# Linear attention, routed experts and a gated layer on one core: the state's product and expert 0's rounding on POOL, sums of decays three units ahead

## The chip, the cores and the metric

The kernel runs on one core of a Trainium2 chip. The metric is device time in microseconds (us), the median of three runs. Five engines work in parallel, each in the order of its own queue: PE (matrix products), DVE (vector work), ACT (functions of one input, copies), POOL (a slower vector engine that also issues indirect transfers) and SP, which only issues transfers. An instruction waits on semaphores for what it reads and for the buffer that it writes.

## The reference

Three layers follow each other; each works on 3072 tokens of 384 numbers.

```python
# 1: linear attention, B=4, H=8, S=768, D=48
f = 1.0 / (1.0 + np.exp(-f_logit))
for t in range(S):
    state = f[:, :, t, :, None] * state + np.einsum('bhd,bhe->bhde', k[:, :, t], v[:, :, t])
    y[:, :, t] = np.einsum('bhd,bhde->bhe', q[:, :, t], state)
# 2: each token goes to the one expert e of 8 with the largest logit
h = np.maximum(x[mask] @ w1[e], 0.0)
out[mask] = gate_w[mask, None] * eom[mask, e, None] * (h @ w2[e])
# 3: gated layer, 1536 wide
out = ((1.0 / (1.0 + np.exp(-(x @ w_gate)))) * (x @ w_val)) @ w_out
```

## The kernel before

**Stages.** The attention is cut into 24 units u of 128 tokens (6 units for each of 4 batches; `c = u % 6` is the place in the batch). After it come nine passes over the experts (expert 0 in two, the second when its late rows have arrived) and then six groups of the gated layer. The order of all engines' work is written out by hand (`manual_schedule`).

**One unit.** The decays `ft` go through Exp and Ln on ACT (`s_log`, `s_log2`), then through a running sum along the tokens on DVE (`s_sum`, L556). `s_keys` takes Exp of the sum on ACT (`gi`, L565) and multiplies the keys by it on DVE (`kT`, L567); `s_queries` takes Exp of the negative sum on ACT (L574) and multiplies the queries by it on POOL (`qT`, L576). `s_end` copies the chunk's whole decay to `gc_all` (L581). `s_score` makes the scores `pS` on PE from kT and qT, `s_mask` masks them on DVE in two halves (`am`, L607), `s_y` makes the output `pY` on PE from am, v, qT and the state, and ACT copies it to `xT`. `s_turn` turns kT on PE (`pk`, copied to `kt` by ACT), `s_state` makes `pM` from kt and v on PE, and DVE adds the old state (L637) and multiplies by the chunk's decay (L638): this is the next state `sn`, made for c = 1 to 4 in these two steps (16 units) and for c = 0 in one (L635). `s_rows` turns xT back on PE (`px`), ACT copies it to rows `x`, and DVE sums the router's logits (`lg`, L505).

**The loop.** Iteration i, from 1 to 23, issues, in this order: scores of unit i, keys and queries of i+1, the load of qk for i+4, `s_end`, rows that POOL puts into the experts' places (`put_rows`, two or three indirect transfers, L385), Exp of the decays of i+2, the load of ft for i+6, masks of i, a step of the routing (`step_route`), output of i-1, Ln of i+2, the load of v for i+4, the state of i, the sum of i+2, the turn of i+1, a step of `feed`, the rows of i-1.

**Loads.** SP issues them in the loop's order: per unit two of qk (48x1024 floats, 192 KB each), two of ft (48x512, 96 KB each) and one of v (128x384, 192 KB). There are 3 buffers of qk, 4 of ft, 5 of v. In iterations 2 to 5 SP also writes two blocks of zeros (`xs_all<-zrow`). `feed` loads expert 0's weights, five tiles ahead (128x512 or 128x2x384 floats: three of 256 KB and two of 384 KB first, from iteration 6), and `split` makes of each 128x512 or 128x384 piece a rounded half `w_hi` on ACT (L243) and the rest `w_lo` on DVE (L244); the loop makes one of the 14 pieces in each iteration from 8 on.

**After the loop.** `make_plan`, a generator of five steps, sorts the experts by size on DVE and PE (L895 to L935); the passes' loop calls it from unit 2 on. Its second step holds a product on PE (`pf`, L904) that reads `chk` of the first. Only then are the next expert's weights loaded.

The two lines that the change moves between engines:

```python
    nc.scalar.copy(hi, src)                                                     # L243, in split
    nc.vector.tensor_tensor(out=sn, in0=sn, in1=gcb, op=ALU.mult)               # L638, in s_state
```

## Time and profile before

| | us |
|---|---|
| runs | 850.44, 854.07, 851.29 |
| median | 851.29 |
| the profiled execution | 854.3 |
| its span, first to last instruction | 852.5 |

The profile is of one execution, 3.0 us above the median; 1.8 us of its time lie around its span. PE is busy for 823.2 us of the span, DVE for 450.2, ACT for 353.5, POOL for 166.9. The attention takes the first 142 us. After that PE is busy in nearly every microsecond, so what moves the end is when PE can begin with the experts, and waits of PE behind that. Times in rows count from the span's start.

### The profile page before, as it was taken

The page shows a single profiled execution, that of the slowest core. Times are in us where ns is not written, and L with a number is a line of the kernel's source. Part 1 is how long each engine was busy: PE and PEld are TensorE (multiplying, and loading weights), DVE is VectorE, ACT ScalarE, POOL GpSimd, SP SyncE. Part 2 cuts the span into 40 slices and gives each one's busy share as a digit, 9 for nine tenths or more (in the row PEclk, how much of TensorE's full clock was granted, in tenths as well). Part 3 has the DMA queues.
Part 4 walks back from the last instruction along what each step waited for, and adds up shares of the span by engine and source line. Part 5 has one row for each costly group of instructions (what it writes and reads, how often), then busy time and mean ns, then how long its engine had stood idle before and what let it go on. Part 6 is the DMA issues. An engine that isn't in the chain of part 4 may idle for free.

```text
span 852.5 us, 13950 instructions
## 1 busy us (share of the span) xinstructions
PE 823.2 (97%) x5289; PEld 727.7 (85%) x5289; DVE 450.2 (53%) x896; ACT 353.5 (41%) x738; POOL 166.9 (20%) x172
## 2 busy tenths in 40 slices
PE   8898989999999999999999999999999999999995
PEld 5776777998899999998888888888888888888884
DVE  6787997568878988997552213222222221232211
ACT  7677874375556665654342212212221221122211
POOL 4225475102323333332000100100010010001001
PEclk9999999999999999999999999999999999999999
DMA  6999762666667767634000200110020010001001
GB/s 158 258 283 266 192 177 82 217 208 196 208 191 224 222 212 218 204 104 139 1 1 1 74 1 1 38 38 0 1 75 1 0 38 2 1 1 38 1 1 40
DMA packets 51645, 87.56 MB, mean 103 GB/s; under 512 B 12874, under 2 KB 32754, under 8 KB 51570
## 3 DMA queue, kind: packets, MB, share of 16 engines
q1 hardware_dynamic: 44946, 62.97, 26.0%
q0 software_dynamic: 6624, 23.62, 8.6%
q8 instruction: 43, 0.70, 0.4%
q14 instruction: 32, 0.26, 0.1%
HBM read 68.35 MB, written 18.22 MB: 102 GB/s over the span
## 4 chain that ended last, share of the span: by engine, by line
issue 51%; PE 32%; DMA 6%; DVE 4%; ACT 3%; POOL 2%; SPq 0%; POOLq 0%; DVEq 0%; ACTq 0%
PE ph L812 5%; PE po L812 5%; PE po L814 5%; PE po L813 5%; PE ph L813 4%; PE ph L814 4%; DMA qk<-in_qkt_dram 4%; POOL out_dram L1022 2%; DMA xs_all<-zrow 1%; DMA ft<-in_ft_dram 1%; PE ptx L430 1%; DVE ls L556 1%; PE pY L653 1%; ACT gi L565 1%; PE px L494 1%
## 5 line engine op out<-in xcount | busy, mean ns | idle before, releaser
L1150 DVE TENSOR_TENSOR hf<-pv,sg 128x512 f32<-128x512 f32 x72 | 49.8, 692 | 266.7 <-PE pv L814 263.1
L1146 ACT ACTIVATE sg<-pg 128x512 f32<-128x512 f32 x72 | 43.1, 598 | 172.8 <-PE pg L814 172.8
L1153 ACT CAST hh<-hf 128x512 fp32r<-128x512 f32 x72 | 44.7, 620 | 161.1 <-DVE hf L1150 152.2
L1022 POOL DMA_INDIRECT out_dram<-ob,ids x24 | 23.6, 983 | 411.4 <-DVE ob L1021 405.9
L813 PE MATMUL po<-w_lo,hh 128*128 128x384 f32 x288 | 96.6, 335 | 0.0
L812 PE MATMUL po<-w_hi,hh 128*128 128x384 f32 x288 | 96.4, 335 | 0.0
L814 PE MATMUL po<-w_hi,hl 128*128 128x384 f32 x288 | 96.3, 334 | 0.0
L814 PE MATMUL pg<-xt_hi,w_lo 128*128 128x512 f32 x216 | 85.5, 396 | 0.0
L813 PE MATMUL pv<-xt_lo,w_hi 128*128 128x512 f32 x216 | 85.5, 396 | 0.0
L812 PE MATMUL pg<-xt_hi,w_hi 128*128 128x512 f32 x216 | 85.5, 396 | 0.0
L813 PE MATMUL pg<-xt_lo,w_hi 128*128 128x512 f32 x216 | 85.1, 394 | 0.0
L812 PE MATMUL pv<-xt_hi,w_hi 128*128 128x512 f32 x216 | 85.1, 394 | 0.0
L814 PE MATMUL pv<-xt_hi,w_lo 128*128 128x512 f32 x216 | 85.1, 394 | 0.0
L244 DVE TENSOR_TENSOR w_lo<-st,w_hi 128x384 fp32r<-128x384 f32 (+1 forms) x112 | 68.9, 647 | 13.9 <-ACT w_hi L243 13.2
L1154 DVE TENSOR_TENSOR hl<-hf,hh 128x512 fp32r<-128x512 f32 x72 | 49.9, 693 | 49.4 <-ACT hh L1153 49.4
L812 PE MATMUL po<-hh,w_hi 128*128 128x192 f32 (+8 forms) x216 | 74.2, 343 | 0.0
L814 PE MATMUL po<-hh,w_lo 128*128 128x192 f32 (+8 forms) x216 | 74.1, 343 | 0.0
L813 PE MATMUL po<-hl,w_hi 128*128 128x192 f32 (+8 forms) x216 | 73.9, 342 | 0.0
L812 PE MATMUL ph<-xt_hi,w_hi 128*128 128x304 f32 (+7 forms) x192 | 67.9, 354 | 0.9 <-DVE hl L1073 0.9
L193 POOL TENSOR_SCALAR cva<-cva 128x512 f32<-128x512 f32 (+1 forms) x30 | 56.3, 1875 | 62.4 <-ACT cva L192 62.1
L1072 ACT ACTIVATE hh<-ph 128x192 fp32r<-128x192 f32 (+8 forms) x72 | 35.6, 494 | 79.1 <-PE ph L814 73.3
L243 ACT CAST w_hi<-st 128x384 fp32r<-128x384 f32 (+1 forms) x112 | 59.3, 558 | 21.9 <-PE po L813 20.0
(173 smaller groups left out, 1658.1 us busy)
## 6 DMA issues: line engine op xcount, KB each, us to landing
st<-in_moe_w_dram SPq DMA_DIRECT2D x48, 256.0 KB
st<-in_moe_w_dram SPq DMA_DIRECT2D x32, 384.0 KB
qk<-in_qkt_dram SPq DMA_DIRECT2D x48, 192.0 KB
ft<-in_ft_dram SPq DMA_DIRECT2D x48, 96.0 KB
v<-in_v_dram SPq DMA_DIRECT2D x24, 192.0 KB
stg<-in_moe_w_gate_dram POOLq DMA_DIRECT2D x9, 512.0 KB
stg<-in_moe_w_val_dram POOLq DMA_DIRECT2D x9, 512.0 KB
stg<-in_moe_w_out_dram POOLq DMA_DIRECT2D x12, 384.0 KB
```

The source lines that it names most:

```text
L193: nc.gpsimd.tensor_scalar(out=af, in0=af, scalar1=HW_LEAST, scalar2=HW_MOST, op0=ALU.max, op1=ALU.min)
L243: nc.scalar.copy(hi, src)
L244: nc.vector.tensor_tensor(out=lo, in0=src, in1=hi.bitcast(F32), op=ALU.subtract)
L812: nc.tensor.matmul(ps, lhsT=ah, rhs=bh, start=first, stop=False)
L813: nc.tensor.matmul(ps, lhsT=ah, rhs=bl, start=False, stop=False)
L814: nc.tensor.matmul(ps, lhsT=al, rhs=bh, start=False, stop=last)
L1022: put = nc.gpsimd.indirect_dma_start(out=out[:, :], out_offset=bass.IndirectOffsetOnAxis(ap=idx[g][:, i : i + 1], axis=0), in_=ob, in_offs ...
L1072: nc.scalar.activation(out=hh, in_=pS, func=AF.Relu)
L1146: nc.scalar.activation(out=sg, in_=pg, func=AF.Sigmoid)
L1150: nc.vector.tensor_tensor(out=hf, in0=pv, in1=sg, op=ALU.mult)
L1153: nc.scalar.copy(hh, hf)
L1154: nc.vector.tensor_tensor(out=hl, in0=hf, in1=hh.bitcast(F32), op=ALU.subtract)
```

## The change

It does these things:

- `s_state`: the product L638 goes from DVE to POOL; the add in front of it stays on DVE.
- `split` gets `steps`. For expert 0 (`r == 0`) it hands back two steps: POOL rounds `w_hi` (instead of ACT), and DVE makes `w_lo` in a later call of `feed.step`. The loop calls two steps in an iteration from 8 on, one in iteration 7.
- `feed.issue()`, the first load of weights, moves from iteration 6 to 5.
- Exp, Ln and running sum work in place in one tile `ls` with four buffers, and from iteration 4 on they run for unit i+3 instead of i+2; iteration 4 does both. The load of ft follows the Exp directly, so that from iteration 4 on it is for i+7.
- `s_end` is for i+1, so that the decay is there when POOL multiplies.
- In the last iteration a step of routing stands ahead of the masks, and the two others behind the rows of unit 22.
- `make_plan` starts one unit of the passes later (no step in unit 2, one in unit 3, then two).

```diff
-            ln = wk.tile([PD, HP, P], F32, name="ln")
-            nc.scalar.activation(out=ln, in_=tin["f", u], func=AF.Exp, scale=-1.0)
+            ls = wk.tile([PD, HP, P], F32, name="ls", bufs=4)
+            nc.scalar.activation(out=ls, in_=tin["f", u], func=AF.Exp, scale=-1.0)
+            load("f", u + NFT)
...
+            (nc.scalar.copy if steps == 1 else nc.gpsimd.tensor_copy)(hi, src)
...
-                    nc.vector.tensor_tensor(out=sn, in0=sn, in1=gcb, op=ALU.mult)
+                    nc.gpsimd.tensor_tensor(out=sn, in0=sn, in1=gcb, op=ALU.mult)
...
-                on(s_end, i)
+                on(s_end, i + 1)
+                if 1 < i <= LEAD:
+                    s_log(i + 2)
+                    s_log2(i + 2)
...
-                if i > 1:
-                    on(s_log, i + 2)
-                    s_mask(i, 0)
-                load("f", i + 6)
+                if i >= LEAD:
+                    on(s_log, i + 3)
+                if i == LAST:
+                    step_route()
+                s_mask(i, 0)
...
-                if i > 1:
-                    on(s_sum, i + 2)
+                if i >= LEAD:
+                    on(s_sum, i + 3)
                 on(s_turn, i + 1)
-                if i == 6:
+                if i == 5:
                     feed.issue()
-                if i >= 8:
-                    feed.step(1)
+                if i >= 7:
+                    feed.step(1 if i == 7 else 2)
...
-                        for _ in range(1 if i == 2 else 2):
+                        for _ in range(min(i - 2, 2)):
```

What stands in a row on the engines, at three places. First SP's queue in iterations 5 to 7, before; `qk_114` is the buffer of unit 9, `qk_115` that of unit 10, `qk_116` that of unit 11.

```order
L539 DMA qk_114<-in_qkt_dram 48x1024 x2
L539 DMA ft_113<-in_ft_dram 48x512 x2
L535 DMA v<-in_v_dram 128x384
L784 DMA xs_all<-zrow 128x2x386 x2
L539 DMA qk_115<-in_qkt_dram 48x1024 x2
L539 DMA ft_110<-in_ft_dram 48x512 x2
L535 DMA v<-in_v_dram 128x384
L252 DMA st_748<-in_moe_w_dram 128x512
L252 DMA st_750<-in_moe_w_dram 128x512
L252 DMA st_752<-in_moe_w_dram 128x512
L259 DMA st_754<-in_moe_w_dram 128x2x384
L259 DMA st_756<-in_moe_w_dram 128x2x384
```

And the same place after:

```order
L555 DMA qk_114<-in_qkt_dram 48x1024 x2
L555 DMA ft_110<-in_ft_dram 48x512 x2
L551 DMA v<-in_v_dram 128x384
L264 DMA st_665<-in_moe_w_dram 128x512
L264 DMA st_667<-in_moe_w_dram 128x512
L264 DMA st_669<-in_moe_w_dram 128x512
L273 DMA st_671<-in_moe_w_dram 128x2x384
L273 DMA st_673<-in_moe_w_dram 128x2x384
L807 DMA xs_all<-zrow 128x2x386 x2
L555 DMA qk_115<-in_qkt_dram 48x1024 x2
```

The five tiles of weights stand ahead of the keys and queries of unit 10 instead of behind them, and one pair of ft loads more stands ahead of them too.

Second, DVE's queue in iterations 14 and 15, before (`SCALAR_TENSOR_TENSOR ls` is the running sum, which the trace calls TENSOR_TENSOR_SCAN):

```order
L172 TENSOR_TENSOR oh<-sc,ms_all 128x48
L637 TENSOR_TENSOR sn<-pM,sn 112x192
L638 TENSOR_TENSOR sn<-sn,gc_all 112x192
L556 SCALAR_TENSOR_TENSOR ls<-runs_108,ln 112x512
L244 TENSOR_TENSOR w_lo<-st_756,w_hi 128x384
L505 TENSOR_REDUCE lg<-px 128x16
L567 TENSOR_TENSOR kT<-qk_114,gi 112x512
```

And after:

```order
L172 TENSOR_TENSOR oh<-sc,ms_all 128x48
L652 TENSOR_TENSOR sn<-pM,sn 112x192
L572 SCALAR_TENSOR_TENSOR ls<-runs_108,ls 112x512
L251 TENSOR_TENSOR w_lo<-st_673,w_hi 128x384
L521 TENSOR_REDUCE lg<-px 128x16
L582 TENSOR_TENSOR kT<-qk_114,gi 112x512
```

The product is gone from between the add and the running sum; the sum is that of a unit one further on.

Third, POOL's queue in iterations 19 to 22, before:

```order
L576 TENSOR_TENSOR qT<-qk_116,ls 112x512
L383 COPY x<-meta 128x2 x2
L385 DMA xs_all<-x,sidx 4096x386 x2
L576 TENSOR_TENSOR qT<-qk_114,ls 112x512
L383 COPY x<-meta 128x2 x3
L385 DMA xs_all<-x,sidx 4096x386 x3
L576 TENSOR_TENSOR qT<-qk_115,ls 112x512
L383 COPY x<-meta 128x2 x2
L385 DMA xs_all<-x,sidx 4096x386 x2
L576 TENSOR_TENSOR qT<-qk_116,ls 112x512
```

And after, where a product and a rounding stand behind the puts of an iteration and ahead of the next queries:

```order
L399 COPY x<-meta 128x2 x2
L401 DMA xs_all<-x,sidx 4096x386 x2
L653 TENSOR_TENSOR sn<-sn,gc_all 112x192
L248 CAST w_hi<-st_1481 128x384
L591 TENSOR_TENSOR qT<-qk_114,ls 112x512
L399 COPY x<-meta 128x2 x3
L401 DMA xs_all<-x,sidx 4096x386 x3
L653 TENSOR_TENSOR sn<-sn,gc_all 112x192
L248 CAST w_hi<-st_1481 128x384
L591 TENSOR_TENSOR qT<-qk_115,ls 112x512
L399 COPY x<-meta 128x2 x2
L401 DMA xs_all<-x,sidx 4096x386 x2
```

## Rows read from the trace of the kernel before

**Rows 1.** Busy time by 10 us: stretch, length, PE, PEld, DVE, ACT, POOL, PEclk, DMA, GB/s.

```profile
40.00:50.00 10.00, 10.00 (x149) 8.93 (x150) 8.04 (x18) 9.04 (x23) 2.61 (x3) 1.00 1.06 289
60.00:70.00 10.00, 8.75 (x132) 7.15 (x130) 8.92 (x25) 7.23 (x20) 2.74 (x2) 1.00 0.94 211
160.00:170.00 10.00, 10.00 (x79) 9.78 (x79) 5.00 (x13) 4.66 (x12) 0.00 (x0) 1.00 0.67 225
```

**Rows 2.** The chain of work that ended last, in order: start, us, what.

```profile
42.70 6.12 DMA qk<-in_qkt_dram
48.83 6.79 DMA qk<-in_qkt_dram
...
57.16 7.63 DMA qk<-in_qkt_dram
64.92 0.69 DVE kT L567
```

**Rows 3.** Timeline of DVE: start, us, line, operation, tiles, [idle before].

```profile
16.66 1.91 DVE L556 TENSOR_TENSOR_SCAN ls<-runs,ln 112x512 f32<-112x512 f32 x1
...
58.98 0.69 DVE L567 TENSOR_TENSOR kT<-qk,gi 112x512 f32<-112x512 f32 x1 [0.27 <-ACT gi L565]
...
85.44 0.35 DVE L637 TENSOR_TENSOR sn<-pM,sn 112x192 f32<-112x192 f32 x1
85.90 0.36 DVE L638 TENSOR_TENSOR sn<-sn,gc_all 112x192 f32<-112x192 f32 x1
86.17 1.22 DVE L556 TENSOR_TENSOR_SCAN ls<-runs,ln 112x512 f32<-112x512 f32 x1
87.31 0.53 DVE L244 TENSOR_TENSOR w_lo<-st,w_hi 128x384 fp32r<-128x384 f32 x1
...
88.09 0.69 DVE L567 TENSOR_TENSOR kT<-qk,gi 112x512 f32<-112x512 f32 x1
88.69 1.28 DVE L607 TENSOR_TENSOR am<-pS,tri 128x512 f32<-128x512 f32 x2
```

**Rows 4.** Busy time between two starts: unit 10's keys to unit 23's; late puts.

```profile
58.98:130.41 71.43, 62.21 (x894) 52.35 (x893) 62.33 (x147) 56.87 (x146) 39.66 (x46) 0.98 0.77 205
104.57:132.36 27.79, 25.06 (x372) 21.18 (x373) 24.98 (x58) 22.69 (x60) 22.13 (x28) 1.00 0.51 148
```

**Rows 5.** Waits of DVE from 58.9 to 130.5 us: in total, times, longest.

```profile
DVE sn L635 <- PE px L494: 3.2, 1, 3.2
DVE ls L556 <- ACT ln L550: 1.2, 2, 0.6
DVE kT L567 <- DMA qk<-in_qkt_dram: 0.6, 1, 0.6
```

**Rows 6.** Timeline of PE: a whole unit, and the plan's product behind the attention.

```profile
40.75 1.16 PE L600 MATMUL pS<-qT,kT 48*128 48x128 f32 x16
...
45.48 1.16 PE L600 MATMUL pS<-qT,kT 48*128 48x128 f32 x16
...
150.85 0.20 PE L904 MATMUL pf<-chk,onec 128*1 128x10 f32 x2 [1.60 <-DVE chk L901]
...
152.31 0.41 PE L813 MATMUL po<-hl,w_hi 128*128 128x192 f32 x1
...
155.81 0.27 PE L813 MATMUL po<-hl,w_hi 128*128 128x192 f32 x1
```

**Rows 7.** Groups of instructions: times, shapes, count | busy, mean ns | idle before.

```profile
L638 DVE TENSOR_TENSOR sn<-sn,gc_all 112x192 f32<-112x192 f32 x16 | 6.1, 382 | 1.9 <-ACT ln L550 0.5
L692 POOL COPY rw<-ident 112x448 f32<-112x448 f32 x1 | 0.6, 557 | 0.1
L193 POOL TENSOR_SCALAR cva<-cva 128x512 f32<-128x512 f32 (+1 forms) x30 | 56.3, 1875 | 62.4 <-ACT cva L192 62.1
```

**Rows 8.** Timeline of POOL: queries under DVE's sum, under its kT, and two puts.

```profile
16.21 1.27 POOL L576 TENSOR_TENSOR qT<-qk,ls 112x512 f32<-112x512 f32 x1 [4.78 <-ACT gc_all L581]
...
65.03 1.71 POOL L576 TENSOR_TENSOR qT<-qk,ls 112x512 f32<-112x512 f32 x1 [4.00 <-ACT gc_all L581]
...
84.90 1.02 POOL L385 DMA_INDIRECT xs_all<-x,sidx  x1 [0.16 <-POOL x L383]
86.22 2.47 POOL L385 DMA_INDIRECT xs_all<-x,sidx  x1 [0.30 <-issue]
```

More of the change, by code (lines that the diff above doesn't have):

```diff
@@ L237, with split, first, second @@
     ring_s = Slots(ring, "ring", NRING)
-    def split(slots, key, src):
+    def split(slots, key, src, steps=1):
         n = src.shape[-1]
-        hi = slots.tile(key, [P, n], F32R, "w_hi")
-        lo = slots.tile(key, [P, n], F32R, "w_lo")
-        nc.scalar.copy(hi, src)
-        nc.vector.tensor_tensor(out=lo, in0=src, in1=hi.bitcast(F32), op=ALU.subtract)
-        pieces[key] = (hi, lo)
+        hi = lo = None
+        def first():
+            nonlocal hi, lo
+            hi = slots.tile(key, [P, n], F32R, "w_hi")
+            lo = slots.tile(key, [P, n], F32R, "w_lo")
+            (nc.scalar.copy if steps == 1 else nc.gpsimd.tensor_copy)(hi, src)
+        def second():
+            nc.vector.tensor_tensor(out=lo, in0=src, in1=hi.bitcast(F32), op=ALU.subtract)
+            pieces[key] = (hi, lo)
+        if steps == 1:
+            first()
+            second()
+        return [first, second]
     def expert_items(r, e):
@@ L254, in w1 @@
             )
+            if r == 0:
+                return split(ring_s, ("w1", r, kk, n), st, 2)
             return [lambda: split(ring_s, ("w1", r, kk, n), st)]
@@ L259, in w2 @@
             nc.sync.dma_start(st, moe_w2[ex, f * P : (f + 2) * P, :].rearrange("o (a p) d -> p (o a) d", p=P))
+            if r == 0:
+                return [s_ for a in range(2) for s_ in split(ring_s, ("w2", r, f + a), st[:, a, :], 2)]
             return [lambda a=a: split(ring_s, ("w2", r, f + a), st[:, a, :]) for a in range(2)]
@@ L542, in s_log @@
         def s_log(u):
[L544 to L546 removed]
+            ls = wk.tile([PD, HP, P], F32, name="ls", bufs=4)
+            nc.scalar.activation(out=ls, in_=tin["f", u], func=AF.Exp, scale=-1.0)
+            st[u] = dict(ls=ls)
+            load("f", u + NFT)
         def s_log2(u):
[L549 to L550 removed]
+            ls = st[u]["ls"]
+            nc.scalar.activation(out=ls, in_=ls, func=AF.Ln, bias=1.0)
         def s_sum(u):
[L554 to L555 removed]
+            ls = st[u]["ls"].rearrange("p h t -> p (h t)")
             nc.vector.tensor_tensor_scan(
[L557 to L558 removed]
+                out=ls, data0=runs01.rearrange("p h t -> p (h t)"), data1=ls, initial=0.0, op0=ALU.mult, op1=ALU.add,
             )
@@ L703 @@
                 s_log2(u)
-                load("f", u + 4)
                 s_sum(u)
@@ L714 @@
             s_end(0)
+            s_end(1)
             s_log(2)
@@ L717 @@
             s_turn(1)
-            load("f", 6)
             load("v", 4)
@@ L747 @@
                 load("qk", i + 4)
-                on(s_end, i)
+                on(s_end, i + 1)
+                if 1 < i <= LEAD:
+                    s_log(i + 2)
+                    s_log2(i + 2)
                 put_rows(2 if i < 19 else 3 if i < 22 else 6)
-                if i > 1:
-                    on(s_log, i + 2)
-                    s_mask(i, 0)
-                load("f", i + 6)
+                if i >= LEAD:
[3 more added lines that the diff above has]
+                s_mask(i, 0)
                 s_mask(i, 1)
-                if i == 1:
+                if i <= LEAD:
                     s_sum(i + 2)
-                step_route()
+                if i < LAST:
+                    step_route()
                 s_y(i - 1)
-                if i > 1:
-                    on(s_log2, i + 2)
+                if i >= LEAD:
+                    on(s_log2, i + 3)
                 load("v", i + 4)
                 s_state(i)
-                if i > 1:
-                    on(s_sum, i + 2)
+                if i >= LEAD:
+                    on(s_sum, i + 3)
                 on(s_turn, i + 1)
-                if i == 6:
+                if i == 5:
                     feed.issue()
-                if i >= 8:
-                    feed.step(1)
+                if i >= 7:
+                    feed.step(1 if i == 7 else 2)
                 if i == LAST:
+                    s_y(i)
                     scale(xg[0], passes[0][2], nc.vector)
-                    s_y(i)
-                for _ in range(2 if i == LAST else i > 16):
+                elif i > 16:
                     step_route()
                 s_rows(i - 1)
+                if i == LAST:
+                    step_route()
+                    step_route()
                 for u0, n in groups:
```

8 lines of the change are left out of this document (1 added, 7 removed).

## The prediction

> **What bounds the kernel now.** I read the busy time by stretches first: behind the attention PE is busy for all of 10 us in 10 [rows 1], so the end moves with the time at which PE gets there, and with waits of PE after it. Inside the attention I follow the keys kT, since unit 10's begin at 58.98 us [rows 3], unit 11's at 64.92 [rows 2], and unit 23's at 130.41 [rows 4].
>
> Up to unit 11 the loads are the limit. In the chain of waits three loads of qk take 6.12, 6.79 and 7.63 us from issue to landing [rows 2], and the transfer engines are busy all the time at 40 to 50 us (share 1.06, 289 GB/s) and nearly so at 60 to 70 [rows 1]. The last part of unit 10's qk lands at 48.83 + 6.79 = 55.62 us, 3.4 us before it is used; that of unit 11 at 57.16 + 7.63 = 64.79, and kT starts at once [rows 2].
>
> From there to unit 23 DVE is the limit: busy for 62.33 of 71.43 us in 13 units, where ACT has 56.87 and POOL 39.66 [rows 4]; a good part of the rest is gaps of a tenth between dependent instructions. Its longest wait, 3.2 us, is for PE [rows 5]. PE itself needs 45.48 - 40.75 = 4.73 us for a whole unit in which it waits for nothing [rows 6], against 71.43 / 13 = 5.49 in this stretch [rows 4]: about 0.76 us a unit can be had at most, 10 us in all.
>
> **The change part by part.**
>
> *Weights one iteration earlier.* SP's queue now has the five tiles of weights (3 x 256 + 2 x 384 = 1536 KB) and one pair of ft (192 KB) ahead of unit 10's qk. Rate: between the two landings (9.17 us) the queue carried ft and v of one unit, the weights and qk, 192 + 192 + 1536 + 384 = 2304 KB, so 251 KB per us. 1728 KB take 6.9 us, and unit 10's qk lands at 55.62 + 6.9 = 62.5 us, 3.5 us later than its kT began. What units 3 to 9 gain before that (their sums come earlier, five products are gone) is waited away there. Lowest: 0, if the queue has room that the shares of 1.06 and 0.94 hide. Highest: 6.9, if kT would have to wait for other late loads as well. I take **+3.5**. After it unit 11's qk stands no later than before but for the one pair of ft (0.8 us), and no longer binds.
>
> *The product off DVE.* 16 of them, 382 ns each [rows 7]; 9 lie between 58.98 and 130.41. In the row of a unit the add starts at 85.44, the product at 85.90, the sum at 86.17 [rows 3]; without the product the sum can start 0.27 after the add (the distance from product to sum), so 0.45 us go per unit: 9 x 0.45 = **-4.1**. Those of units 1 to 9 are hidden behind the loads.
>
> *Sums three units ahead.* From 58.9 us on DVE waited 1.2 us for Ln ahead of the sum and 0.6 us for a load [rows 5]; both go: **-1.8**. Nothing more hangs on it, as DVE is the limit there, and a sum that is ready early does not shorten DVE's own queue.
>
> *POOL's new work beside DVE.* The product has no row on POOL. The same kind of instruction on 112x512 takes 1.27 us there [rows 8] and 0.69 on DVE [rows 3]; 192 columns by the same share of columns are 0.48, by DVE's 0.36 times the ratio 1.84 they are 0.66; I take 0.55 as an estimate. The rounding lies between a plain copy of 112x448 (0.557, so 0.64 for 512) and L193, two operations on up to 512 columns (1.88 on average) [rows 7]; I take 0.64, as the copy is the nearer kind. What they cost shows where two engines meet: the running sum took 1.91 instead of 1.22 us when POOL's qT had started 0.45 us before it [rows 3, 8], qT took 1.71 instead of 1.27 when kT had started first [rows 2, 8], and a put, 1.02 alone, took 2.47 when it started 0.05 after the running sum, as if it could only begin behind w_lo [rows 3, 8]. So the product, which is released just as DVE starts the sum, waits until w_lo ends, and then kT, due about 0.3 us later, waits for what is left of it, 0.25 us: 9 x 0.25 = +2.2. The rounding then falls beside the masks, which read PSUM. The next qT follows it and ends near the start of the next sum in units without routing work, five of the 13: 5 x 0.3 = +1.5. Together **+3.7**; lowest 0 (product and rounding fall into DVE's gaps), highest 14 x 0.64 + 9 x 0.55 = 13.9 (all in DVE's way).
>
> The Trainium skill (SBUF — State Buffer, "SBUF: two separate sides") says that VectorE with two SBUF inputs and a GpSimd operation that reads SBUF hold one pair of ports exclusively, for the whole instruction. By that rule a put would also hold back DVE; but kT took its usual 0.69 at 88.09 while the put of 86.22 ran until 88.69 [rows 3, 8], so here the puts pay and DVE doesn't. For the product and the roundings trace and rule would agree on who waits, not on how long the queue behind them gets.
>
> *POOL's late puts.* From 104.57 to 132.36 us POOL is busy for 22.13 of 27.79 us [rows 4], the rest mostly the 0.3 us in front of each put. The change adds four roundings and three products there, 4 x 0.64 + 3 x 0.55 = 4.2 us. Of the 5.7 us of rest some 2.8 can take it up, so qT of unit 23 comes **+1.5** later; lowest 0, highest 4.2.
>
> *ACT.* It loses 14 roundings; at 56.87 of 71.43 us it isn't the limit [rows 4]. Nothing.
>
> *The tail.* The first routing step of the last iteration now runs while DVE waits for the scores, but the product that the rank needs comes later on PE, behind the rows of unit 22. I set them against each other: 0.
>
> *The plan one unit later.* PE waits 1.60 us for `chk` ahead of `pf`, and then some 15 products start 0.21 us apart rather than 0.11 (0.41 against 0.27 long) [rows 6], at half the granted clock; 1.5 us. Now a unit of PE's work lies between. If the wait goes wholly, 3.1 us; if `chk` itself is a unit later and still late, 0.7. I take **-2.4**. The loads of the next expert start some 2 us later; PE runs without a wait for long after [rows 1], so they cost nothing as long as they land in time.
>
> **The sum.** +3.5 - 4.1 - 1.8 + 3.7 + 1.5 - 2.4 = +0.4 us. From the profiled 854.3 that is 854.7; the median lies 3.0 below the profiled execution, so 851.7, rounded to 851.5.
>
> **The rivals.**
>
> *Faster: loads have room, locks are cheap.* The queue takes the weights without delaying unit 10 (0 for +3.5), and POOL's work falls into DVE's gaps (+1.0 for +5.2). For it: 3.4 us of slack at unit 10, and PE's 4.73 us a unit, well below 5.49. Sum: -4.1 - 1.8 + 1.0 - 2.4 = -7.3, so 844.0. Against it: the share of 1.06, and kT that starts 0.13 us behind its load.
>
> *Slower: POOL becomes the bound.* The rounding costs on POOL what L193 costs, 1.88 instead of 0.64: 4 x 1.24 = 5.0 us more in the stretch where POOL has no rest, and in 9 earlier units it runs into the next sum, 9 x 0.3 = 2.7. It decides from about 1.2 us on, where product, rounding and qT no longer fit beside the masks. Sum: 0.4 + 5.0 + 2.7 = +8.1, so 859. The Trainium skill (GPSIMD Engine Reference, "Engine selection") calls one-input operations on GpSimd roughly line-rate, which speaks against this price; no row here shows a rounding.
>
> *The lead does nothing.* DVE waits for other inputs wherever it waited for Ln, so the 1.8 us stay: 853.5, still within the bound of no change.
>
> **How the numbers follow.** A measurement here tells 0.5%, 4.3 us, from no change. The forecast, with the third rival, holds times from 847 to 855.5: chance 0.46. The faster rival 0.28, the slower one 0.26. The likeliest case's own range is 848 to 855; for 8 in 10 it reaches half way into each rival, 844.5 to 858.5.
>
> **What would show it.** Right: unit 10's kT waits for a load until about 62.5 us; the interval from there to unit 23's kT is shorter than 71.43; kT after a product lasts more than 0.69; POOL has no rest from the second group of puts on; the wait ahead of `pf` is under 1 us. Wrong: unit 10's kT starts before 59 us without a wait for a load (then the first rival), or a rounding on POOL lasts over 1.2 us (then the second).

## The result, and the profile of the changed kernel

The changed kernel takes 864.12 us (median of four runs, 862.84 to 867.82), the kernel before 851.76 us in the same session (850.44 to 854.07). The ratio is 1.0149, interval 1.011 to 1.0189. The forecast was 851.5 us and its range ended at 858.5: it was wrong by 12.6 us, and on the slower side. The profiled execution took 867.82 us with a span of 866.1, against 854.3 and 852.5 before.

Where the 13.5 us between the two profiled executions arose can be read from a few starts. Unit 10's keys are 0.55 us later than before (59.53 for 58.98), unit 23's 5.3 us (135.69 for 130.41), PE's first product of the passes 10.1 us (152.67 for 142.54), and the end of the span 13.6 us. So 4.7 us are lost between unit 10's keys and unit 23's, 4.9 from there to the first pass, and 3.5 in the passes. The last of these is less sure than the others: from PE's first product of the passes to the end it is 713.4 us here and 710.0 before, but in six other profiled kernels whose passes are those of the kernel before it ranges from 708.1 to 712.1.

Busy time of the changed kernel by stretches, in the columns of [rows 1] and [rows 4]:

```profile
50.00:60.00 10.00, 5.96 (x111) 4.88 (x102) 5.33 (x10) 5.77 (x16) 4.90 (x5) 0.96 1.06 315
60.00:70.00 10.00, 9.72 (x81) 8.50 (x82) 8.61 (x23) 4.23 (x10) 6.03 (x5) 0.50 1.01 230
160.00:170.00 10.00, 8.68 (x39) 7.96 (x40) 4.21 (x24) 0.88 (x3) 2.96 (x4) 0.58 0.63 209
59.53:135.69 76.16, 64.39 (x869) 55.13 (x871) 65.67 (x137) 51.12 (x126) 61.68 (x65) 0.88 0.72 186
104.57:132.36 27.79, 21.25 (x329) 17.99 (x324) 25.38 (x52) 17.28 (x44) 25.60 (x28) 1.00 0.52 136
```

Three things stand out beside [rows 1] and [rows 4]. POOL is busy for 61.68 us of the 13 units instead of 39.66, and for 25.60 of the 27.79 us of the late puts instead of 22.13. DVE is busy for 65.67 us instead of 62.33, though a product of every unit was taken from it. And the granted clock is at its lower level (1.2 GHz, shown as 0.50) for all of 60 to 70 us, where it was 1.00 before, after PE had been busy for 5.96 of 10 us.

Rows of DVE's timeline (start, duration, line, operation, tiles, idle time before):

```profile
59.53 0.69 DVE L582 TENSOR_TENSOR kT<-qk,gi 112x512 f32<-112x512 f32 x1 [4.64 <-DMA qk<-in_qkt_dram]
...
94.64 1.41 DVE L582 TENSOR_TENSOR kT<-qk,gi 112x512 f32<-112x512 f32 x1
...
113.26 1.61 DVE L172 TENSOR_TENSOR oh<-sc,ms_all 128x40 bf16<-128x40 f32 x1
...
119.36 1.31 DVE L365 SCALAR_TENSOR_TENSOR pf<-ms_all,rk 128x5 f32<-128x5 f32 x1
```

And POOL's at the same places:

```profile
93.08 1.87 POOL L653 TENSOR_TENSOR sn<-sn,gc_all 112x192 f32<-112x192 f32 x1 [0.66 <-DVE sn L652]
94.90 0.60 POOL L248 CAST w_hi<-st 128x512 fp32r<-128x512 f32 x1
95.47 1.72 POOL L591 TENSOR_TENSOR qT<-qk,ls 112x512 f32<-112x512 f32 x1
...
113.07 0.52 POOL L248 CAST w_hi<-st 128x384 fp32r<-128x384 f32 x1
113.54 1.27 POOL L591 TENSOR_TENSOR qT<-qk,ls 112x512 f32<-112x512 f32 x1
...
115.21 2.41 POOL L401 DMA_INDIRECT xs_all<-x,sidx  x1 [0.17 <-POOL x L399]
```

The keys at 94.64 take 1.41 us where they took 0.69 [rows 3]: the product on POOL ends at 94.95 and the rounding holds on until 95.50. A routing instruction of 0.20 us (`oh` at 113.26) lasts 1.61, until qT on POOL is done at 114.81; `pf` at 119.36, 0.17 by itself, lasts until the qT of 119.38 is done. These are two-input instructions on DVE; that they stand still while POOL works is read from these starts and ends. In the kernel before, qT began 0.77 us behind the keys in nearly every unit from 12 to 21 and so ran beside the masks, which read PSUM; nothing was stretched there.

Last, waits of PE from 59 to 145 us (in total, times, longest), one of DVE from 59.4 to 135.7, and the first product of the passes in PE's timeline:

```profile
PE pS L615 <- POOL qT L591: 8.2, 6, 3.4
PE pk L603 <- DVE kT L582: 5.3, 2, 3.5
```

```profile
DVE ls L572 <- ACT ls L567: 3.6, 2, 3.4
```

```profile
152.67 0.35 PE L835 MATMUL ph<-xt,w_hi 128*128 128x192 f32 x1 [1.86 <-DVE xt L428]
```

PE waits 8.2 us for POOL's queries; before, it had waited for them once, 0.42 us. Its waits for the keys add up to 5.3 us in both kernels. DVE's wait for Ln, which the lead of three units was to remove, is 3.6 us instead of 1.2 [rows 5]. And PE waits 1.86 us for `xt` ahead of the first pass.

### The profile page after: what moved, and what is told of

Read it like the earlier page. It is cut to its first block, busy times and chain, and to the rows that moved or that the text cites. A ratio compares the mean times of both kernels' runs of the same rounds, so it can differ in the third digit from the quotient of the medians.

```text
span 866.1 us, 13902 instructions
## 1 busy us (share of the span) xinstructions
PE 831.4 (96%) x5289; PEld 735.3 (85%) x5289; DVE 452.4 (52%) x880; ACT 350.6 (40%) x724; POOL 196.8 (23%) x202
## 4 chain that ended last, share of the span: by engine, by line
issue 51%; PE 35%; DVE 4%; POOL 4%; DMA 3%; ACT 2%; SPq 0%; POOLq 0%; DVEq 0%; ACTq 0%
PE ph L835 5%; PE po L835 5%; PE ph L837 5%; PE ph L836 5%; PE po L837 5%; PE po L836 5%; POOL out_dram L1045 2%; DMA qk<-in_qkt_dram 2%; PE px L510 1%; PE pY L668 1%; PE pS L615 1%; PE ptx L446 1%; DVE am L622 1%; DMA ft<-in_ft_dram 1%; DVE ls L572 1%
## 5 line engine op out<-in xcount | busy, mean ns | idle before, releaser
L836 PE MATMUL ph<-xt_lo,w_hi 128*128 128x304 f32 (+7 forms) x192 | 67.1, 349 | 0.0
```

The costliest lines, as they stand in the source:

```text
L836: nc.tensor.matmul(ps, lhsT=ah, rhs=bl, start=False, stop=False)
```

## The experiments

Eighteen kernels ran. Two theories stood at the start. Theory POOL: the product and the roundings on POOL stand in DVE's way and make the queries late. Theory clock: the early weights bring the stall of 4.64 us at unit 10, PE's clock falls, and that is the loss.

Two numbers go with every kernel below. "Stretched" is, from unit 10's keys to 5 us after unit 23's in the profiled execution, the time that DVE's instructions took beyond the usual time of the same operation and tile (the 30th percentile over all kernels), counted where it is over 0.15 us, in one execution of each kernel; the 6.4 us that an expectation names for the lead were counted from unit 3 on and a little differently. "Low clock" is twice the share missing from the mean granted clock times the span, the time at 1.2 GHz, as a mean over the runs; it was 33 us in the changed kernel and 18 in 108 runs of the kernel before.

| kernel | us | before | ratio (interval) | stretched | low clock |
|---|---|---|---|---|---|
| before | | 851.76 | 1 | 0.5 | 18 |
| the change | 864.12 | 851.76 | 1.0149 (1.011 to 1.0189) | 8.7 | 33 |
| change, product on DVE | 866.84 | 849.87 | 1.018 (1.013 to 1.0231) | 8.0 | 43 |
| change, roundings on ACT | 861.53 | 849.87 | 1.0117 (1.007 to 1.0164) | 8.8 | 28 |
| change, both back | 865.58 | 849.87 | 1.0181 (1.0131 to 1.0232) | 5.9 | 35 |
| change, weights late | 861.42 | 849.87 | 1.014 (1.0063 to 1.0217) | 14.3 | 35 |
| lead, end and plan alone | 861.15 | 851.35 | 1.0093 (1.006 to 1.0126) | 5.0 | 32 |
| lead alone | 858.03 | 851.35 | 1.0063 (1.003 to 1.0096) | 5.9 | 28 |
| lead, queries behind the keys | 857.32 | 852.05 | 1.0069 (1.0035 to 1.0102) | 6.8 | 23 |
| end alone | 856.18 | 851.35 | 1.0044 (1.0017 to 1.007) | 0.3 | 28 |
| end, two steps only | 851.93 | 848.54 | 1.0029 (1.0007 to 1.0051) | 2.2 | 22 |
| end, pause of PE filled | 851.80 | 848.40 | 1.0045 (1.0024 to 1.0066) | 2.2 | 17 |
| plan alone | 852.03 | 851.35 | 1.0002 (0.9981 to 1.0024) | 0.8 | 19 |
| early weights alone | 851.27 | 852.05 | 0.9996 (0.9974 to 1.0018) | 0.6 | 19 |
| product on POOL alone | 852.38 | 852.05 | 1.0011 (0.9988 to 1.0033) | 1.7 | 21 |
| these three together | 848.35 | 848.54 | 0.9987 (0.9972 to 1.0003) | 1.7 | 16 |
| roundings on POOL, same step | 865.89 | 852.05 | 1.0162 (1.0128 to 1.0196) | 5.1 | 37 |
| roundings on POOL, a tile ahead | 856.89 | 848.54 | 1.0091 (1.0064 to 1.0118) | 8.8 | 24 |
| change without lead and end | 860.33 | 848.54 | 1.0141 (1.0107 to 1.0174) | 13.0 | 28 |
| product on POOL below unit 18, plan | 848.93 | 848.40 | 0.9985 (0.9966 to 1.0004) | 1.0 | 19 |

### Taking parts back out of the change

The product back on DVE, the roundings back on ACT, both, and the weights one iteration later:

```diff
-                    nc.gpsimd.tensor_tensor(out=sn, in0=sn, in1=gcb, op=ALU.mult)
+                    nc.vector.tensor_tensor(out=sn, in0=sn, in1=gcb, op=ALU.mult)
...
-            (nc.scalar.copy if steps == 1 else nc.gpsimd.tensor_copy)(hi, src)
+            nc.scalar.copy(hi, src)
...
-                if i == 5:
+                if i == 6:
                     feed.issue()
-                if i >= 7:
-                    feed.step(1 if i == 7 else 2)
+                if i >= 8:
+                    feed.step(1 if i == 8 else 2)
```

Product on DVE:

> The changed kernel with the product of state and decay back on DVE; all else as changed. Theory POOL (the new work on POOL holds up DVE and the queries): the keys no longer wait for the product (9 times about 0.7 us between units 10 and 23), DVE gets 9 x 0.38 us back as work, and POOL loses products of up to 2.0 us each in its queue, so that the queries of the last units come earlier: about 858 us instead of 864. Theory clock (the stall for unit 10's load, brought by the early weights, lowers the granted clock for 17 us, and that is the loss): nothing changes at the stall, 863 to 865 us, and the clock is still 0.5 between 60 and 75 us.

Roundings on ACT:

> The changed kernel with the roundings of expert 0's weights back on ACT; all else as changed. Theory POOL: POOL loses 14 x 0.6 = 8.5 us of work between 64 and 135 us, PE's wait for the queries (9.0 us in all) shrinks to some 3 us, about 859 us. Theory clock: 863 to 865 us, the clock still 0.5 between 60 and 75 us.

Both:

> The changed kernel with the product on DVE and the roundings on ACT; the early weights, the sums three units ahead, the end of the attention and the plan stay as changed. Theory POOL: nearly all of the loss goes, 850 to 854 us. Theory clock: the stall at unit 10 and the 17 us at the lower clock stay, 858 to 862 us.

Weights late:

> The changed kernel with the weights issued and split one iteration later, as in the kernel before; product and roundings stay on POOL. Theory POOL: the keys of units 11 to 23 still wait for POOL, and the load wait goes: at most 2 us better, 862 to 864 us. Theory clock: no stall of 4.6 us at unit 10, the clock stays at 1.0 between 60 and 75 us, and half of 17 us comes back less what waits elsewhere: 856 to 858 us.

Measured: 866.84, 861.53, 865.58 and 861.42 us. Neither theory got its number. With product and roundings both back, the loss stays whole (1.0181), so theory POOL falls as the only cause; with the weights late the loss stays as well (1.014), so theory clock in its first form falls too. The profiles say the same: from 60 to 75 us the granted clock is 0.88 or 0.89 in all four and 0.50 in the change, and the loss is there all the same. One reading is that something that stayed in all four kernels is enough for most of the loss, and the lead, the end and the plan stayed in all of them. The other is that several parts are enough each by themselves. Taking parts out can't tell these apart.

### One part alone in the kernel before

The lead alone moves the sums, the place of `s_end` and the loads of ft as the change does; its core:

```diff
-                if i > 1:
-                    on(s_log, i + 2)
-                    s_mask(i, 0)
-                load("f", i + 6)
+                if i >= LEAD:
+                    on(s_log, i + 3)
+                s_mask(i, 0)
...
-                if i > 1:
-                    on(s_sum, i + 2)
+                if i >= LEAD:
+                    on(s_sum, i + 3)
```

The end alone, with the output of the last unit ahead of the scaling, which is part of the change too:

```diff
+                if i == LAST:
+                    step_route()
                 s_mask(i, 0)
...
-                step_route()
+                if i < LAST:
+                    step_route()
                 s_y(i - 1)
...
                 if i == LAST:
-                    scale(xg[0], passes[0][2], nc.vector)
                     s_y(i)
-                for _ in range(2 if i == LAST else i > 16):
+                    scale(xg[0], passes[0][2], nc.vector)
+                elif i > 16:
                     step_route()
                 s_rows(i - 1)
+                if i == LAST:
+                    step_route()
+                    step_route()
```

> The kernel before with the sums three units ahead alone (ls in place of ln, four buffers, ends of decays and loads of ft where the change has them); product on DVE, roundings on ACT, weights, end of the attention and plan as before. What is left of the loss when product and roundings go back lies in the lead, the early weights, the end of the attention or the plan. Theory lead: DVE's queue gets the sum of a later unit ahead of the keys that are due, units 10 to 23 take no less than 71.4 us, and the pauses of PE bring more time at the lower clock: 855 to 860 us. Theory end: the lead costs nothing or gains up to 2 us: 848 to 851 us.

> The kernel before with the new order at the end of the attention alone (the first routing step ahead of the masks, the last product ahead of the scaling of the gathered rows, two routing steps behind the rows of unit 22). Theory end: in the changed kernel PE waits 1.9 us for xt ahead of the first pass, in the kernel before it did not; that wait returns here, and a longer stretch at the lower clock behind it: +2 to +5 us, 852 to 855 us. Theory lead: nothing, 849 to 851 us.

The plan alone:

```diff
-                        for _ in range(1 if i == 2 else 2):
+                        for _ in range(min(i - 2, 2)):
```

> The kernel before with the plan one unit of the pass later alone. As predicted: the wait of 1.6 us ahead of pf goes, and the stretch at the lower clock behind it, 2.4 us less, 847 to 848.5 us. Theory end: the wait goes, but the clock falls elsewhere in the first pass all the same: 849 to 851 us.

And the three of them without the rest, which is the change with all the edits of the section above taken back (`split` keeps its two steps, so that ACT rounds a tile ahead of DVE's difference):

> The changed kernel with product on DVE, roundings on ACT and the weights issued and split one iteration later: of the change only the lead, the end of the attention and the plan are left. Theory clock by early weights: no stall at unit 10, 850 to 853 us. Theory lead and end: 856 to 862 us, as far from the kernel before as with the early weights.

Measured: lead 1.0063, end 1.0044, plan 1.0002, the three together 1.0093. The lead and the end each cost, and together about their sum. The predicted gain of the plan isn't there: PE's wait ahead of `pf` is gone, but in its place PE waits for the scaled rows of the next pass,

```profile
PE ptx L430 <- DVE xs L441: 1.8, 1, 1.8
```

(waits of PE from 140 to 165 us with the plan alone; in the kernel before that wait did not occur there).

In the run with the lead alone, one thing that changed shows in the timelines of POOL and of DVE:

```profile
99.15 1.96 POOL L591 TENSOR_TENSOR qT<-qk,ls 112x512 f32<-112x512 f32 x1 [4.13 <-ACT ls L589]
103.54 1.27 POOL L591 TENSOR_TENSOR qT<-qk,ls 112x512 f32<-112x512 f32 x1 [2.44 <-PE pS L615]
```

```profile
100.03 1.63 DVE L582 TENSOR_TENSOR kT<-qk,gi 112x512 f32<-112x512 f32 x1
...
103.74 1.10 DVE L392 TENSOR_TENSOR carry<-carry,ct 128x8 bf16<-128x8 bf16 x1
```

With the sums three units ahead, ACT has the two exponentials ready long before DVE gets to the keys, so in six of the ten units from 12 to 21 qT starts 0.3 to 3.7 us ahead of kT, not 0.77 us behind it. Five of these keys take about 1.63 instead of 0.69 us, and a `carry` of 0.17 takes 1.10. By these rows the wait that the lead took away had also set POOL's pace. Whether that is what costs the 5 us is the next question.

In the run with the end alone, DVE ahead of the passes and PE at their start:

```profile
139.36 0.23 DVE L505 TENSOR_REDUCE lg<-px 128x16 f32<-128x64 f32 x1 [2.90 <-PE ptx L430]
```

```profile
142.66 0.36 PE L819 MATMUL ph<-xt,w_hi 128*128 128x192 f32 x1 [1.86 <-DVE xt L412]
```

DVE stands for 2.90 us in front of the sum of unit 22's logits, with the two routing steps and `xt` queued behind it, and PE waits for `xt`.

### Does the queries' early start cost the time?

The lead alone, with one more wait:

```diff
+            tc.add_manual_dep(
+                query.ins, d["key"].ins.name,
+                mybir.DependencyInfo(mybir.DependencyClass.Sync, mybir.DependencyReason.DATA), reason="keys first",
+            )
```

> The kernel before with the sums three units ahead alone, and in addition the product of the queries on POOL waits for the product of the keys on DVE. With the lead alone qT started up to 1.8 us ahead of kT (in the kernel before 0.77 us behind it in nearly every unit), and such a kT took 1.63 instead of 0.69 us. Theory collision: every kT takes 0.69 us again, the stretched instructions of DVE between units 3 and 23 fall from 6.4 to about 1 us, and the loss of the lead goes: 849 to 852 us. Theory order (the sum of a later unit stands ahead of the keys in DVE's queue, and ACT's order, cost the time): 856 to 858 us, as with the lead alone.

Measured: 857.32 us, 1.0069, no better; this is the number of theory order. In the profiled execution a part of theory collision holds: the keys of units 10 to 22 take 0.68 us again, and from unit 10's keys to unit 23's it is 68.44 us, where the lead alone had 78.95 and the kernel before 71.43 [rows 4]. The rest of it doesn't: unit 23's keys take 2.10 us, the stretched time is 6.8 us where the lead alone had 5.9, and the last scores end 10.2 us behind unit 23's keys instead of 4.4. Almost one microsecond of this is the lower clock itself: the granted clock is 0.54 on average from 135 to 145 us, and the last scores take 2.08 us instead of 1.16. One row of POOL and one wait of PE (20 to 150 us) in this kernel bear on it:

```profile
103.94 1.88 POOL L399 COPY x<-meta 128x2 int32<-128x2 int32 x2
```

```profile
PE pS L619 <- POOL qT L591: 7.3, 6, 2.9
```

In nine of the 14 units from 10 on qT now starts 0.90 to 1.01 us behind the keys instead of 0.77 and ends just behind the masks; the two copies of a put, 0.30 us in the kernel before, then fall under DVE's sum and take 1.88. In the other five qT is 2.85 to 4.74 us late, and PE waits 7.3 us for queries. By these rows the collision was moved rather than removed. But the total is also what theory order forecast, and no run parts the two: that the lead costs is shown, by which of the two ways is not. That the 0.2 us of later start alone turn the copies was not tested by itself either.

### Early weights, product and roundings alone

```diff
-                if i == 6:
+                if i == 5:
                     feed.issue()
-                if i >= 8:
+                if i >= 7:
                     feed.step(1)
```

> The kernel before with the weights of expert 0 issued and split one iteration earlier, alone. By the prediction's step the load of unit 10 comes 3.5 us later than its keys: +3.5 us, 854 to 856 us, with a wait of the keys for qk of 3 to 4 us and a stretch at the lower clock behind it. Rival: the queue has room, 850 to 852 us and no wait at unit 10.

The product alone is the one line of the first edit above, the other way round:

> The kernel before with the product of state and decay on POOL, alone. Prediction: DVE gets 0.45 us a unit, POOL takes back 0.25: -2 us, 848.5 to 850.5 us. Rival: the product is released as the sum begins and can start only behind it and w_lo, takes 2.0 us, and kT 1.41 instead of 0.69: +0.3 us a unit and a later qT, 853 to 858 us.

The roundings on POOL, once in the step of the difference that uses them, and once a tile ahead, with the change's `split` at the time of the kernel before:

```diff
-        nc.scalar.copy(hi, src)
+        (nc.gpsimd.tensor_copy if key[1] == 0 and key[0] in ('w1', 'w2') else nc.scalar.copy)(hi, src)
```

```diff
                 if i >= 8:
-                    feed.step(1)
+                    feed.step(1 if i == 8 else 2)
```

> The kernel before with the roundings of expert 0's weights on POOL, alone, in the same step as the difference that uses them. Prediction: 0.6 us a tile, beside the masks, nothing until the late puts, then +1.5 us: 851 to 853 us. Rival: the rounding stands in the way of kT or the sum in every unit, and the difference waits for it: 854 to 860 us.

> The kernel before with the roundings on POOL one tile ahead of the differences that use them, as in the change, but at the time of the kernel before; nothing else. With the rounding in the same step as its difference the loss was 14 us. Theory chain: that loss was DVE waiting for w_hi behind POOL's queue; with a tile of lead the wait is gone, 851 to 854 us. Theory POOL load: the 14 roundings push POOL's puts into DVE's sum and keys and the queries of the last units come late all the same, 856 to 866 us.

Measured: weights 0.9996, product 1.0011, roundings 1.0162 and 1.0091. The weights alone got the rival's number, and in their profile the wait of 3 to 4 us for unit 10's load is not there, as DVE's timeline shows:

```profile
58.85 0.69 DVE L567 TENSOR_TENSOR kT<-qk,gi 112x512 f32<-112x512 f32 x1 [0.71 <-ACT ls L574]
```

The 0.71 us that are there are put down to ACT's Exp for the queries, which the keys don't read; they may be the load.

The product at 852.38 us lies between its two forecasts. The roundings are the one part of these that costs, and of all parts the dearest; in the same step they cost more than either forecast. There DVE waits for the rounded halves (59 to 140 us):

```profile
DVE w_lo L244 <- POOL w_hi L243: 11.4, 7, 4.5
```

A tile ahead that wait is 0.3 us, and a loss of 0.91% is left, 856.89 us, in the range of theory POOL load. So theory chain holds for a part at most. The price of one rounding was as predicted, 0.49 to 0.62 us where nothing holds it up. What the roundings do beyond that wait is to be seen, with the roundings a tile ahead, in the timelines of POOL and of DVE, in a wait of PE and in the busy time of 10 us:

```profile
77.06 0.58 POOL L248 CAST w_hi<-st 128x384 fp32r<-128x384 f32 x1
77.61 1.25 POOL L592 TENSOR_TENSOR qT<-qk,ls 112x512 f32<-112x512 f32 x1
...
82.20 0.51 POOL L248 CAST w_hi<-st 128x384 fp32r<-128x384 f32 x1
82.67 1.26 POOL L592 TENSOR_TENSOR qT<-qk,ls 112x512 f32<-112x512 f32 x1
```

```profile
77.67 1.61 DVE L251 TENSOR_TENSOR w_lo<-st,w_hi 128x384 fp32r<-128x384 f32 x1 [0.33 <-POOL w_hi L248]
...
82.05 1.96 DVE L169 TENSOR_TENSOR sc<-lg,m 128x48 f32<-128x48 f32 x1
```

```profile
PE pS L616 <- POOL qT L592: 5.3, 4, 2.1
```

```profile
80.00:90.00 10.00, 7.92 (x122) 6.86 (x120) 9.52 (x18) 5.63 (x15) 9.22 (x11) 1.00 0.81 222
```

In this stretch of puts POOL has hardly any rest (9.22 of 10 us). The rounding stands ahead of the next queries, so qT starts 4.00 and 3.33 us behind the keys of units 13 and 14 (0.77 before), out of the masks' cover, and DVE's `w_lo` (0.53 alone) and `sc` (0.20 alone) take 1.61 and 1.96 us: the first lasts until qT is done, the second until rounding and qT are. PE waits 5.3 us for queries between 20 and 150 us.

### Which move at the end, and is it the clock?

Only the two routing steps behind the rows of unit 22:

```diff
-                for _ in range(2 if i == LAST else i > 16):
+                if 16 < i < LAST:
                     step_route()
                 s_rows(i - 1)
+                if i == LAST:
+                    step_route()
+                    step_route()
```

> The kernel before with only the two routing steps of the last iteration put behind the rows of unit 22. In the run with the whole new end DVE waited 2.9 us for px of unit 22, with the routing steps and xt queued behind it, and PE waited 1.86 us for xt ahead of the first pass. Theory steps: this move alone does it, the waits return and the time is 854 to 857 us. Rival: the other moves (the first step ahead of the masks, the product ahead of the scaling) are needed for it, 850.5 to 852.5 us.

Measured: 851.93 us, 3.4 above the kernel before in its own session (848.54), and 1.86 us of waiting for `xt` again. The two steps bring the wait; with a ratio of 1.0029 and an interval of 1.0007 to 1.0051 they may be all of the end's cost or half of it.

Then the whole end, with matmuls in the pause:

```diff
             s_rows(LAST)
+            keep_warm(8)
```

> The kernel before with the whole new end (3.9 us slower by the mean of its runs, with 8 us more at the lower clock), and in addition eight matmuls of 128x512 on a constant, whose result nothing uses, in the 1.86 us in which PE waits for xt ahead of the first pass. They do no work for the result. Theory clock: what the end costs is mostly the lower clock after that pause; with PE busy in it the low stretch of the first pass goes back to that of the kernel before and the loss shrinks from about 4 to 1 to 2 us. Theory wait: the pause itself and the later routing cost the time; the matmuls change nothing, +3.5 to +4.5 us.

PE's timeline in that kernel:

```profile
137.60 1.89 PE L311 MATMUL pw<-oneb 128*128 128x512 bf16 x8
139.62 0.36 PE L820 MATMUL ph<-xt,w_hi 128*128 128x192 f32 x1
```

The pause is filled, and the time at the lower clock is only 2 us above that of the kernel before in the same session, where the end without the matmuls had 8 more. The ratio does not follow: 1.0045, as without, which is 3.8 us and the number of theory wait. Theory clock doesn't get its number here either (a loss of 1 to 2 us would be a ratio of 1.0024 at most, the lower end of the interval). The intervals of the two runs are too wide to say that nothing at all came back.

### Is the rest additive, and is anything worth keeping?

Weights, product and plan together are the three edits shown for each; the change without lead and end adds its `split` for the roundings. The last kernel is the plan and

```diff
-                    nc.vector.tensor_tensor(out=sn, in0=sn, in1=gcb, op=ALU.mult)
+                    (nc.gpsimd if u < 18 else nc.vector).tensor_tensor(out=sn, in0=sn, in1=gcb, op=ALU.mult)
```

> The kernel before with the three parts that cost nothing alone: weights one iteration earlier, product on POOL, plan one unit later. Theory additive: 851 to 853 us, as before. Rival: they disturb each other (the stall at unit 10 with fewer products before it, POOL's product in front of the puts), 855 to 858 us. A gain, under 849 us, would need DVE's freed 0.45 us a unit to reach the end.

> The whole change without the sums three units ahead and without the new order at the end: early weights, product and roundings (one tile ahead) on POOL, plan one unit later. Theory additive: the lead (+6) and the end (+4) together make up 9 to 10 of the 13 us, so 854 to 856 us remain. Theory POOL load: the roundings alone make up the loss, 860 to 866 us. Theory lead: everything but the lead and the end is free, 850 to 853 us.

> A version that might beat both: the kernel before with the product on POOL for the units below 18 alone and the plan one unit later; weights, sums, roundings and end as before. Up to unit 18 POOL has room and units 10 to 19 take less time; the last units, where POOL's puts hold back the queries, keep the product on DVE. Theory gain: 1 to 3 us less than before. Rival: what the keys gain is waited away by PE at the end of the attention, no difference within 1 us.

Measured: 0.9987, 1.0141 and 0.9985. The three parts that are free alone are free together, though unit 10's keys then wait 4.11 us for their load and the clock falls there as well, as DVE's timeline and the busy time of 10 us of these three show:

```profile
61.57 0.69 DVE L567 TENSOR_TENSOR kT<-qk,gi 112x512 f32<-112x512 f32 x1 [4.11 <-DMA qk<-in_qkt_dram]
```

```profile
59.00:69.00 10.00, 9.84 (x121) 8.27 (x118) 7.23 (x19) 5.31 (x14) 4.64 (x3) 0.65 0.90 224
```

But this profile is of the slowest of the kernel's twelve runs (850.77 us at a mean clock of 0.987; the others took 847.42 to 849.9 at 0.989 to 0.993), and the time at the lower clock over all twelve, 16 us, is that of the kernel before. So the stall at unit 10 with the lower clock behind it, the most visible thing in the profile of the change, may be in this execution alone; that it costs nothing is not shown, only that the early weights as a whole cost nothing here. Adding the roundings to these three brings the loss from -0.1% to +1.4%, which is as much as the whole change loses, without lead and end. No version beat the kernel before by more than its interval.

## Why the prediction was wrong, point by point

*Early weights (+3.5).* The term was mis-sized. In the changed kernel unit 10's keys do wait for their load, 4.64 us, and what units 3 to 9 had gained (2.85 us at unit 9: 49.62 for 52.47) is waited away there. But the load came by 59.53, not 62.5. With the weights alone the keys start at 58.85, so it had landed by then, at most 3.2 us later than at 55.62 and not the 6.9 that the prediction made of one rate. Alone the part costs nothing (0.9996), nor together with product and plan (0.9987).

*Product off DVE (-4.1) and on POOL (+2.2).* The product takes 0.51 us when nothing is in its way and 1.87 to 2.12 when it is released into the sum, as the prediction said. Alone it gives 1.0011. Part of the gain is visible, 66.46 us from unit 10's keys to unit 23's, where four other profiled kernels that change nothing there on DVE or POOL (plan, early weights, and the end with two steps or with the pause filled) have 67.4 to 68.0; the kernel before has 71.43 and the end alone 71.46, both with a stretch at the lower clock between. In the kernel before this is the row

```profile
70.00:80.00 10.00, 8.55 (x96) 7.31 (x98) 6.15 (x11) 7.22 (x18) 7.30 (x10) 0.83 1.05 268
```

and DVE's wait of 3.2 us for PE [rows 5] ends just behind it, at 80.25. So 3.4 to 4 of the 71.43 us were of that one execution, and with 67.4 to 68.0 us a unit takes 5.2 us, not 5.49: what could be had was nearer 6 us in all than the 10 of the prediction.

What the product gains is gone by the end: qT of unit 23 starts 3.34 us behind its keys instead of 1.95, and PE waits 1.8 us for it. The step that failed is that a shorter queue on DVE would reach the end.

*Sums three units ahead (-1.8).* This step failed outright: "Nothing more hangs on it" was wrong. Alone the lead costs 0.63%, 5.4 us of 851.76, instead of giving 1.8. By the rows the wait for the sum had kept ACT's exponentials, and with them POOL's queries, behind the keys; but putting the queries behind the keys again brought nothing back (1.0069), so whether the cost is that or the order on DVE and ACT stays open.

*Roundings on POOL (part of +3.7, and +1.5 for the late puts).* This is the term that was most mis-sized. The price of one was right (0.60 for 512 columns against 0.64). Its place was wrong: "beside the masks" held only where no puts stood in the queue in front of it. Behind puts the rounding comes ahead of the next queries and, by the rows, pushes them out of the masks' cover into DVE's two-input instructions. Measured alone, a tile ahead: 0.91%, 7.8 us, and 1.54%, some 13 us, where product, early weights and plan are there too (1.0141 against 0.9987).

*The port.* The prediction read from one put that POOL pays and DVE doesn't. That was a put; with arithmetic on POOL, DVE pays, at `oh` (1.61 for 0.20) and kT (1.41 for 0.69). The Trainium skill (SBUF — State Buffer, "SBUF: two separate sides") says that whichever of the two starts first holds the shared ports for the whole instruction and the other is blocked; the products, roundings and copies on POOL here agree in both directions (2.00 for 0.51 us for the product on POOL, 1.61 for 0.20 for `oh` on DVE). The put that the prediction set against it is another matter: in the 20 profiles, of 458 two-input instructions of DVE without PSUM that began while a put alone ran on POOL, seven took 0.2 to 0.4 us longer than usual and the others their usual time. What a put showed did not hold for arithmetic.

*The slower rival.* At 859 it was the nearest of the forecasts, and POOL did come near to having no rest. But it was tied to a rounding of 1.2 us and more; here one took 0.6. With the late puts at 22.13 of 27.79 us [rows 4] and gaps of 0.3 us in front of each put, there was little room for half a microsecond per unit.

*ACT (0).* Nothing speaks against it: roundings back on ACT are no slower (1.0117 against 1.0149).

*The end (0).* It costs 0.44% alone. The failed step is "I set them against each other": the two steps that were moved stand behind a wait of 2.90 us for PE, with `xt` behind them.

*The plan (-2.4).* 1.0002 alone. The wait of 1.60 us went, but 1.8 us of waiting for the next rows took its place.

*The signs.* Of the signs of being right, keys of 1.41 us behind a product, POOL without rest in the late puts (25.60 of 27.79 us) and the end of the wait ahead of `pf` came; the load at 62.5 us and an interval below 71.43 us (it is 76.16) did not. Of the signs of being wrong neither came: unit 10's keys waited for a load, and no rounding took more than 0.77 us. The rivals didn't cover what happened, since none had the lead or the end as a cost, or the roundings at their own price.

The whole: lead, end and roundings each cost by themselves, 0.63, 0.44 and 0.91%. The three don't add. Roundings with the three free parts make 1.41%, lead and end with the plan 0.93%, and all together 1.49%. So the first series could not show a culprit: whichever part is taken out, the others are enough for most of the loss. What goes with it is DVE held up by POOL: all kernels with 5.0 us or more of stretched instructions lose 0.6% or more, and all with 2.2 us or less lose nothing measurable, but for those with the new end, whose cost lies behind that stretch. The amount does not follow, though: 14.3 us go with 1.4%, 5.1 with 1.62%. That each of the three parts costs is shown by runs; that the way is POOL's hold on DVE is read from rows, and the one run that was to undo it, for the lead, did not.

Three things stay open. The early weights cost nothing alone, but lead, end and plan are 1.0093 without them and 1.0181 with them; why, no run tells. And how the 12 us divide among lead, end and roundings when all are there can't be said, as the parts overlap. Last, the clock: lead, end and roundings (a tile ahead) each have about 8 us more at the lower clock than the kernel before in their sessions. At the 0.36 us for each such us that the last section gives, that would be an estimated 3 us, of 5.7, 3.6 and 7.6 by the means of the runs. Filling the pause at the end took most of these 8 us away without a gain, so the clock may only go along with PE's waits; no run tells for the other two.

## What to carry to other kernels

When two engines can hold each other up, ask of every wait you remove whether it also kept them out of each other's way; here the same product on POOL took 0.51 us when nothing stood in its way and 1.87 to 2.12 us when it met DVE's sum. An engine at 80% in a stretch of fixed-order work, as POOL was with 22.13 of 27.79 us, can have no room for a small instruction in front of one that others wait for. One profiled execution can hold some us that are its own: compare a stretch over several kernels that don't touch it before you plan with it. And if a change has several parts, run each alone in the old kernel, not only the change without it: two sufficient causes hide each other.

## What was not expected of the hardware

Runs of the same kernel differ by up to 13 us over all sessions, and with it goes PE's time at its lower clock level: over 267 runs of 20 kernels, 0.36 us (standard error 0.02) for each us at 1.2 GHz, compared within a kernel. The kernel before alone ranged from 846.2 us with 12 us at the lower level to 859.5 with 34. Still, filling a pause of 1.86 us ahead of the passes took some 6 us of it away and left the ratio at 1.0045. How much of the 0.36 the clock makes, and how much is PE's pauses that lower it, stays open.

An instruction of 40 columns on DVE, 0.20 us by itself, took 1.6 us when it met two instructions of POOL in a row; a put's two copies of 2 columns each took 1.88 us together instead of 0.30 under DVE's sum. At such places the size of an instruction said little of what it cost.
